# Turning a list schedule over, and squares' sums on VectorE alone, in a fused attention and GLU kernel

## The chip, the cores and the metric

The kernel runs on one core of one Trainium2 chip. The metric is device time in microseconds (us), the median over several executions. A core has a matrix engine (TensorE, PE), a vector engine (VectorE, DVE), an activation engine (ScalarE, ACT), GpSimd (POOL) and SyncE (SP), which here only issues transfers (DMAs). Each engine takes its instructions in the order in which the program lists them; they wait for one another through semaphores.

## The reference

The first part is attention over channels for 4 batches of 6080 tokens and 256 channels; the second a gated layer on its output with 2048 hidden channels.

```python
def _attn_ref(q, k, v, tau):
    qn = q / (np.linalg.norm(q, axis=1, keepdims=True) + 1e-06)
    kn = k / (np.linalg.norm(k, axis=1, keepdims=True) + 1e-06)
    s = kn.transpose(0, 2, 1) @ qn / tau
    s = s - s.max(-1, keepdims=True)
    a = np.exp(s)
    a /= a.sum(-1, keepdims=True) + 1e-09
    return (v @ a).astype(np.float32)

def _moe_ref(x, w_in, w_out):        # x: the rows of all batches
    h = x @ w_in
    g = h * (1.0 / (1.0 + np.exp(-1.702 * h)))
    return (g @ w_out).astype(np.float32)
```

`q`, `k`, `v` are float32, `w_in` and `w_out` arrive as 64-bit floats.

## The kernel before

The norms run over the tokens, so the scores of a batch need one pass over `q` and `k`, and the squares' sums of all columns come from the same pass. The softmax's 256x256 matrix is multiplied into `w_in`, so that each batch has its own weights (`weights`), and the long work is then one gated layer on `v`.

*The long work.* Tokens are cut into chunks of up to 1024, six for a batch. A chunk goes through 8 *pairs* of hidden blocks, so there are 4 x 6 x 8 = 192 pairs. A pair has a *front* (products of `w` and `v` into the PSUM banks X, Y, Z, copies of ACT that seed one bank from another, the gates) and a *back* (the gates' high and low parts `gi`, `gj`, `gr` times `wo`, `wb`, into the banks O2, O3, O4, O7 and K). Both use a scheme of seven products in the place of eight; every product is three matmuls, of high and low parts. The very first chunk has another division (`FIRST`) than the rest.

*Before it.* The 64-bit weights are converted on ACT and DVE (`win_convert`, `wout_convert`): the words of one piece are loaded into a buffer (the first ones into `ga0`, `ga1`, `gi0`, `gi1`, the 12 later ones all into `vr`, which `values` uses for `v` too), ACT copies, DVE puts the number together in several steps, and the result is stored to DRAM. Each buffer serves one user after another.

*Scores and squares.* `Attention.unit` handles 2 tiles of 128 tokens of `q` and `k`; a batch has 25 units. It loads them (`raw`), lets PE add to the scores, and lets ACT square them into a buffer `sq` (`gp` for batch 1), which is added into `acc`. Batches 0 and 1 are scored in float32 from `raw`; batches 2 and 3 load a second, rounded copy by POOL's queue (`hl`) and let DVE make the low part. In batch 0 the sum is split, half on DVE, half on POOL; in the other batches POOL issues a DMA that adds `sq` to `acc` (L498). Batch 0 is scored at the start and batch 1 beside the first chunk; batches 2 and 3 are spread over the pairs 19 to 60 and 74 to 118.

*The order.* Every step is a node with an engine, a cost, a *lag* after it (the time until a transfer has landed), what it depends on, the buffers that it uses, and a due time (`due`), worked out by hand from the pair's place. `Plan.order` places the nodes by their modelled times: on each engine, when it comes free, the ready node with the earliest due is next. A node of another engine is ready 60 ns after what it waits for, 165 ns more behind PE, and 350 ns more where PE itself waits. The nodes are then emitted by their start. A buffer's next user waits for all users of the one before. `load` costs 50 ns and 2.6 ns a KB on SP, with a lag of 3000 ns; `load_cast`, on POOL, 800 ns and the same lag.

Of the kernel before, what the change touches and what calls it, by code (L numbers as in the profile page):

```python
# [15 lines left out]
ALU = mybir.AluOpType  # L16
# [34 lines left out]
class Plan:  # L51

    DRAIN = {"PE": 165}
    MARGIN = {"PE": 350}
    HOP = 60

    def __init__(self):
        self.nodes = []  # L60
# [12 lines left out]
        self.nodes.append(n)  # L73
        return n

    def stuck(self):
        seen, path = set(), []
        n = next(n for n in self.nodes if n.start is None)
        while id(n) not in seen:
            seen.add(id(n))  # L80
            path.append((n.idx, n.eng, n.due, [getattr(b, "slot", "") for b in n.uses]))
            n = next(d for d in n.deps if (d.start is None if d.eng is not None else d.left))
        return path[-30:]

    def order(self):
        nodes = self.nodes
        free_of = {}
        extra = []
        for n in nodes:
            n.outs = []  # L90
        for n in nodes:
            deps = {id(d): d for d in n.deps}
            for b in n.uses:
                prev = b.prev
                while prev is not None and not prev.users:
                    prev = prev.prev
                if prev is not None:
                    r = free_of.get(id(prev))
                    if r is None:
                        r = Node(None, 0, None, prev.users, (), 0, 0, -1)  # L100
                        r.outs = []
                        free_of[id(prev)] = r
                        extra.append(r)
                    deps[id(r)] = r
            n.deps = list(deps.values())
        for n in nodes + extra:
            n.left, n.ready = len(n.deps), 0.0
            for d in n.deps:
                d.outs.append(n)
        engines = {n.eng for n in nodes}  # L110
        waiting = {e: [] for e in engines}
        avail = {e: [] for e in engines}
        free = {e: 0.0 for e in engines}
        events = []

        def arrive(n):
            heapq.heappush(waiting[n.eng], (n.ready, n.idx, n))
            heapq.heappush(events, (max(n.ready, free[n.eng]), n.eng))

        def done(n, end):  # L120
            for o in n.outs:
                if o.eng is None:
                    o.ready = max(o.ready, end)
                else:
                    t = end
                    if n.eng is not None and o.eng != n.eng:
                        t += self.DRAIN.get(n.eng, 0)
                    if n.eng != o.eng:
                        t += self.HOP + self.MARGIN.get(o.eng, 0)
                    o.ready = max(o.ready, t)  # L130
                o.left -= 1
                if o.left == 0:
                    if o.eng is None:
                        done(o, o.ready)
                    else:
                        arrive(o)

        for n in nodes:
            if n.left == 0:
                arrive(n)  # L140
        for r in extra:
            assert r.left
        placed = []
        while events:
            t, e = heapq.heappop(events)
            if free[e] > t:
                if waiting[e] or avail[e]:
                    heapq.heappush(events, (free[e], e))
                continue
            while waiting[e] and waiting[e][0][0] <= t:  # L150
                _, _, n = heapq.heappop(waiting[e])
                heapq.heappush(avail[e], (n.due, n.idx, n))
            if not avail[e]:
                continue
            _, _, n = heapq.heappop(avail[e])
            n.start = t
            placed.append(n)
            free[e] = t + n.cost
            done(n, t + n.cost + n.lag)
            if waiting[e] or avail[e]:  # L160
                heapq.heappush(events, (free[e], e))
        if len(placed) != len(nodes):
            raise AssertionError(self.stuck())
        return sorted(placed, key=lambda n: (n.start, n.idx))


def act(n, psum=False):
# [24 lines left out]
def channel_attention_then_glu(  # L192
# [10 lines left out]
    nc = tc.nc  # L203
# [18 lines left out]
    g = Plan()  # L222
# [34 lines left out]
    def plain(ap):  # L257
        return ap.bitcast(F32) if ap.dtype == F32R else ap

    def load(dst, src, kb, deps=(), uses=(), due=0.0):  # L260
        return g.add(
            "SP", 50 + kb * 2.6, lambda: nc.sync.dma_start(plain(dst()), plain(src())), deps, uses, due, lag=3000,
        )

    def load_cast(dst, src, kb, deps=(), uses=(), due=0.0):
        return g.add("POOL", 800, lambda: nc.gpsimd.dma_start(dst(), src()), deps, uses, due, lag=3000)

    def cast(dst, src, n, deps, uses, due, psum=False):
        return g.add("ACT", act(n, psum), lambda: nc.scalar.copy(dst(), src()), deps, uses, due)  # L269
# [4 lines left out]
    def tt(dst, a, b, op, n, deps, uses, due, eng="DVE"):  # L274
        if eng == "POOL":
            return g.add("POOL", pool(n), lambda: nc.gpsimd.tensor_tensor(dst(), a(), b(), op=op), deps, uses, due)
        return g.add("DVE", dve(n), lambda: nc.vector.tensor_tensor(dst(), a(), b(), op=op), deps, uses, due)  # L277
# [144 lines left out]
    class Attention:  # L422
# [39 lines left out]
        def unit(self, u, due, after=()):  # L462
            t0, nt, pp = self.units[u]
            if t0 not in self.raw:
                t = sbuf(f"ra{u % 2}", [P, 2, UT, C], F32, "raw")
                view = (lambda i: t()[:, i, :nt, :]) if pp == P else (lambda i: t()[:pp, i, 0, :])
                ns = [
                    load(
                        lambda i=i: view(i), lambda i=i: self.rows(i, t0, nt, pp), 128 * nt, after, [t], due - 8,
                    )  # L470
                    for i in range(2)
                ]
                for o in range(nt):
                    self.raw[t0 + o] = (t, o, ns)
            buf, o, _ = self.raw[t0]
            ready = [n for j in range(nt) for n in self.raw[t0 + j][2]]
            w = 2 * nt * C
            src = lambda: buf()[:pp, :, o : o + nt, :]
            acc = self.acc
            if u == 0:  # L480
                self.acc_n = [g.add(
                    "ACT", act(w), lambda: nc.scalar.activation(acc(), src(), AF.Square), ready, [buf, acc], due + 0.5,
                )]
            else:
                sq = sbuf("gp" if self.b == 1 else "sq", [P, 2, UT, C], F32, "sq")
                s = g.add(
                    "ACT", act(w),
                    lambda: nc.scalar.activation(sq()[:pp, :, :nt, :], src(), AF.Square), ready, [buf, sq], due + 1,  # L488
                )
                parts = [("DVE", slice(0, 1)), ("POOL", slice(1, 2))] if self.b == 0 else [("DMA", slice(0, 2))]  # L490
                new = []
                for e, (eng, sl) in enumerate(parts):
                    a = lambda sl=sl: acc()[:pp, sl, :nt, :]
                    more = lambda sl=sl: sq()[:pp, sl, :nt, :]
                    deps = [s, self.acc_n[min(e, len(self.acc_n) - 1)]]
                    if eng == "DMA":
                        new.append(g.add(
                            "POOL", 1200, lambda a=a, more=more: nc.gpsimd.dma_start(a(), more(), accum_op=ALU.add),  # L498
                            deps, [sq, acc], due + 1.5, lag=3500,
                        ))  # L500
                    else:
                        new.append(tt(a, a, more, ALU.add, w // len(parts), deps, [sq, acc], due + 1.5, eng))
                self.acc_n = new
            if self.direct:
                op, ok, uses = buf, ready, [buf]
            else:
                hl = sbuf("hl", [P, 2, UT, 2, C], F32R, "hl")
                hs = [
                    load_cast(
                        lambda i=i: hl()[:, i, :nt, 0, :] if pp == P else hl()[:pp, i, 0, 0, :],  # L510
                        lambda i=i: self.rows(i, t0, nt, pp), 128 * nt, after, [hl], due - 6,
                    )
                    for i in range(2)
                ]
                l = low(
                    lambda: hl()[:pp, :, :nt, 1, :], src, lambda: hl()[:pp, :, :nt, 0, :], w,
                    hs + ready, [buf, hl], due,
                )
                ok, uses = [l], [hl]
# [624 lines left out]
```

## Time and profile before

| | us |
|---|---|
| median of 3 runs | 2345.29 |
| lowest and highest | 2343.35, 2357.74 |
| the profiled execution | 2346.11 |
| its span, first to last instruction | 2344.4 |
| PE busy | 2184.9 (93%) |
| DVE busy | 1650.3 (70%) |
| ACT busy | 1583.5 (68%) |
| POOL busy | 179.3 (8%) |
| moved by DMA | 534.86 MB, mean 228 GB/s |

The page gives each engine's busy time and the chain of work that ended last; the table by stage gives the same busy times for stretches of the span, with the granted clock of PE as a share of 2.4 GHz. PE is the engine with most work, but not evenly: in the first 300 us its busy share is far below that of the end. Rows of the trace give the start of an instruction in us from the start of the span, its duration, and in brackets the idle time of its engine before it with what ended it.

### The profile page before, as it was taken

The numbers are of one execution on the slowest core, as the hardware profiler recorded it, in microseconds if no ns is written. First come the engines' busy times: TensorE is split into PE (matmuls) and PEld (weight loads), VectorE is DVE, ScalarE is ACT, GpSimd is POOL, SyncE is SP. The second block draws the span as 40 slices with busy tenths as digits, with TensorE's granted clock in tenths as the row PEclk, the third lists the DMA queues.
The fourth block names the chain that finished last, engine by engine and source line by source line (L and its number), as shares of the span: only waits on it lengthen the run. The fifth ranks groups of instructions, "written<-read, shape, count | busy, mean of one in ns | idle before, by whom it ended". The sixth has DMA issues, their size and how long they took to land.

```text
span 2344.4 us, 27182 instructions
## 1 busy us (share of the span) xinstructions
PE 2184.9 (93%) x9832; PEld 1789.5 (76%) x9832; DVE 1650.3 (70%) x2079; ACT 1583.5 (68%) x2309; POOL 179.3 (8%) x206
## 2 busy tenths in 40 slices
PE   8577699999999999999999999999999999999999
PEld 7455477778777777788787777778888878888887
DVE  6555477676766776877766777678777767767775
ACT  4454477667766676777666676677777777777775
POOL 4301100011111110001111111100000000000000
PEclk9798899999999999999999999999999999999999
DMA  8789867787878876678867878676766555645553
GB/s 287 220 255 270 266 221 250 243 267 235 267 225 255 254 202 207 243 257 266 262 207 245 250 227 257 204 228 215 265 225 215 172 189 193 215 158 203 199 178 127
DMA packets 205108, 534.86 MB, mean 228 GB/s; under 512 B 16688, under 2 KB 74672, under 8 KB 203952
## 3 DMA queue, kind: packets, MB, share of 16 engines
q1 hardware_dynamic: 168304, 472.44, 57.3%
q0 software_dynamic: 36672, 60.70, 12.7%
q8 instruction: 78, 1.28, 0.2%
q14 instruction: 54, 0.44, 0.1%
HBM read 430.44 MB, written 66.85 MB: 212 GB/s over the span
## 4 chain that ended last, share of the span: by engine, by line
PE 63%; DMA 20%; DVE 7%; ACT 6%; issue 2%; POOL 1%; SPq 1%; DVEq 0%; ACTq 0%
PE ps_o L767 21%; PE ps_X L767 12%; PE ps_k L767 9%; PE ps_Y L767 9%; PE ps_Z L767 8%; DMA acc<-sq 5%; DMA hl<-in_k 4%; DMA raw<-in_k 4%; PE ps_s L537 2%; DMA out_T<-oc 2%; ACT ga L793 2%; PE ps_w L684 2%; ACT sq L488 1%; DMA wi<-win_d 1%; DMA v_raw<-in_vT 1%
## 5 line engine op out<-in xcount | busy, mean ns | idle before, releaser
L767 PE MATMUL ps_X<-v,w 128*128 128x512 f32 (+1 forms) x1728 | 495.7, 395 | 14.4 <-ACT ps_Z L269 14.1
L767 PE MATMUL ps_o<-gi,wo 128*128 128x512 f32 (+1 forms) x1752 | 460.1, 389 | 1.7 <-DVE gi L292 1.7
L767 PEld LDWEIGHTS ps_X<-v,w 128*128 128x128 f32 x1728 | 322.7, 190 | 89.7 <-ACT ps_Z L269 29.2
L767 PEld LDWEIGHTS ps_o<-gi,wo 128*128 128x128 f32 x1752 | 328.4, 188 | 69.1 <-DVE gi L292 2.9
L767 PE MATMUL ps_Y<-v,w 128*128 128x512 f32 (+1 forms) x1152 | 331.9, 397 | 25.6 <-ACT ps_Y L269 22.5
L767 PE MATMUL ps_Z<-v,w 128*128 128x512 f32 (+1 forms) x1152 | 328.1, 392 | 22.8 <-ACT w L269 16.1
L793 ACT ACTIVATE ga<-ga 128x512 f32<-128x512 f32 (+1 forms) x384 | 232.9, 625 | 162.7 <-DVE ga L277 161.3
L767 PE MATMUL ps_o<-gj,wo 128*128 128x512 f32 (+1 forms) x1152 | 312.3, 396 | 14.4 <-DVE gj L283 5.4
L292 DVE TENSOR_TENSOR gi<-ga,gi 128x1536 fp32r<-128x1536 f32 (+2 forms) x192 | 280.6, 1462 | 49.3 <-ACT gi L269 48.4
L767 PEld LDWEIGHTS ps_Z<-v,w 128*128 128x128 f32 x1152 | 216.5, 189 | 75.3 <-ACT w L269 19.5
L767 PEld LDWEIGHTS ps_Y<-v,w 128*128 128x128 f32 x1152 | 216.9, 192 | 73.1 <-ACT ps_Y L269 26.8
L767 PEld LDWEIGHTS ps_o<-gj,wo 128*128 128x128 f32 x1152 | 216.6, 191 | 69.8 <-DVE gj L283 16.4
L277 DVE TENSOR_TENSOR ga<-ps_Y,m 128x512 f32<-128x512 f32 (+1 forms) x192 | 131.0, 682 | 183.6 <-PE ps_Y L767 149.1
L269 ACT CAST gi<-ga 128x1536 fp32r<-128x1536 f32 (+2 forms) x192 | 238.9, 1244 | 4.4
L488 ACT ACTIVATE sq<-raw 128x1024 f32<-128x1024 f32 (+1 forms) x96 | 98.2, 1023 | 181.7 <-DMA acc<-sq 73.5
L269 ACT COPY ps_Y<-ps_X 128x512 f32<-128x512 f32 (+1 forms) x192 | 109.3, 570 | 120.4 <-PE ps_X L767 119.2
L283 DVE SCALAR_TENSOR_TENSOR gj<-ga,gj 128x1024 fp32r<-128x1024 f32 (+1 forms) x100 | 121.2, 1212 | 76.4 <-ACT gj L852 76.0
L767 PE MATMUL ps_k<-gj,wo 128*128 128x512 f32 (+1 forms) x600 | 155.6, 390 | 2.6 <-DVE kc L277 1.8
L767 PE MATMUL ps_k<-gr,wb 128*128 128x512 f32 (+1 forms) x552 | 145.9, 388 | 0.0
L269 ACT COPY m<-ps_Z 128x512 f32<-128x512 f32 (+1 forms) x192 | 110.4, 575 | 39.1 <-PE ps_Z L767 39.0
L277 DVE TENSOR_TENSOR ga<-ps_X,m 128x512 f32<-128x512 f32 (+1 forms) x192 | 130.7, 681 | 5.6 <-PE ps_X L767 5.5
L793 ACT ACTIVATE ga<-ps_Y 128x512 f32<-128x512 f32 (+1 forms) x192 | 112.6, 587 | 30.3 <-PE ps_Y L767 29.4
(120 smaller groups left out, 2864.4 us busy)
## 6 DMA issues: line engine op xcount, KB each, us to landing
w<-w_d SPq DMA_DIRECT2D x184, 896.0 KB, 4.8
wo<-wout_d SPq DMA_DIRECT2D x92, 640.0 KB, 5.3
wo<-wout_d SPq DMA_DIRECT2D x100, 512.0 KB, 6.0
acc<-sq POOLq DMA_DIRECT2D x66, 512.0 KB, 5.9
wb<-wout_d SPq DMA_DIRECT2D x92, 256.0 KB, 4.1
w_d<-wst SPq DMA_DIRECT2D x24, 896.0 KB, 6.3
v_raw<-in_vT SPq DMA_DIRECT2D x20, 1024.0 KB, 8.7
out_T<-oc SPq DMA_DIRECT2D x80, 256.0 KB, 5.4
```

Of the source, the lines that this page charges most:

```text
L269: return g.add("ACT", act(n, psum), lambda: nc.scalar.copy(dst(), src()), deps, uses, due)
L277: return g.add("DVE", dve(n), lambda: nc.vector.tensor_tensor(dst(), a(), b(), op=op), deps, uses, due)
L283: lambda: nc.vector.scalar_tensor_tensor(dst(), in0=a(), scalar=-1.0, in1=b(), op0=ALU.mult, op1=ALU.subtract,),
L292: lambda: nc.vector.tensor_tensor(dst(), src(), hi().bitcast(F32), op=ALU.subtract),
L488: lambda: nc.scalar.activation(sq()[:pp, :, :nt, :], src(), AF.Square), ready, [buf, sq], due + 1,
L537: nc.tensor.matmul(out, lhsT=hl()[:pp, 1, j, l, ci], rhs=hl()[:pp, 0, j, r, :], start=begin and m == 0, stop=True, skip_group_check=True,)
L684: nc.tensor.matmul(pb()[:, i * 2 * P : (i + 1) * 2 * P], lhsT=at.aT()[:, l, j, ci], rhs=wi()[:, m, j, :], start=i == 0 and n == 0, stop=Tr ...
L767: nc.tensor.matmul(dst, lhsT=l(a), rhs=r(b), start=begin and n == 0, stop=True, skip_group_check=True,)
L793: lambda: nc.scalar.activation(dst(), src(), AF.Gelu_apprx_sigmoid, scale=sign), deps, uses, at,
```

## The change

Three things change, and the computation stays the same.

First, the order. `graph` now builds, once, the nodes with their incoming and outgoing arcs and the time of each arc (cost, lag, hops). `place` does the list placing for given arcs and a given key of priority. `order` places the nodes forwards with the dues as keys, as before, and then four times: backwards (arcs reversed, those that ended last first), and forwards again with the starts of the backward placing as keys. Of the five forward placings the one with the earliest end by the model is kept.

Second, the squares' sums: in all batches one add on VectorE over the whole unit, 1024 elements a partition, in the place of the halves on DVE and POOL (batch 0) and of the accumulating DMA (batches 1 to 3).

Third, the lags: 4000 ns for a load (5000 for the `raw` of a unit), 6000 for a `load_cast`; the dues of a unit's loads are 2 and 3 earlier.

```diff
+    TURNS = 4
...
+    def order(self):
+        nodes, ins, outs = self.graph()
+        cost = [n.cost for n in nodes]
+        back_ins = [[(b, w + cost[b] - cost[a]) for b, w in x] for a, x in enumerate(outs)]
+        back_outs = [[(a, w + cost[b] - cost[a]) for a, w in x] for b, x in enumerate(ins)]
+        start, end = self.place(nodes, ins, outs, [n.due for n in nodes])
+        best = (end, start)
+        for _ in range(self.TURNS):
+            back, end = self.place(nodes, back_ins, back_outs, [-t - c for t, c in zip(start, cost)])
+            start, end = self.place(nodes, ins, outs, [end - t - c for t, c in zip(back, cost)])
+            best = min(best, (end, start), key=lambda x: x[0])
+        for n, t in zip(nodes, best[1]):
+            n.start = t
+        return sorted(self.nodes, key=lambda n: (n.start, n.idx))
...
-    def load(dst, src, kb, deps=(), uses=(), due=0.0):
+    def load(dst, src, kb, deps=(), uses=(), due=0.0, lag=4000):
...
-        return g.add("POOL", 800, lambda: nc.gpsimd.dma_start(dst(), src()), deps, uses, due, lag=3000)
+        return g.add("POOL", 800, lambda: nc.gpsimd.dma_start(dst(), src()), deps, uses, due, lag=6000)
...
-                        lambda i=i: view(i), lambda i=i: self.rows(i, t0, nt, pp), 128 * nt, after, [t], due - 8,
+                        lambda i=i: view(i), lambda i=i: self.rows(i, t0, nt, pp), 128 * nt, after, [t], due - 10, 5000,
...
-                parts = [("DVE", slice(0, 1)), ("POOL", slice(1, 2))] if self.b == 0 else [("DMA", slice(0, 2))]
-                new = []
-                for e, (eng, sl) in enumerate(parts):
-                    a = lambda sl=sl: acc()[:pp, sl, :nt, :]
-                    more = lambda sl=sl: sq()[:pp, sl, :nt, :]
-                    deps = [s, self.acc_n[min(e, len(self.acc_n) - 1)]]
-                    if eng == "DMA":
-                        new.append(g.add(
-                            "POOL", 1200, lambda a=a, more=more: nc.gpsimd.dma_start(a(), more(), accum_op=ALU.add),
-                            deps, [sq, acc], due + 1.5, lag=3500,
-                        ))
-                    else:
-                        new.append(tt(a, a, more, ALU.add, w // len(parts), deps, [sq, acc], due + 1.5, eng))
-                self.acc_n = new
+                a = lambda: acc()[:pp, :, :nt, :]
+                self.acc_n = [tt(
+                    a, a, lambda: sq()[:pp, :, :nt, :], ALU.add, w, [s, *self.acc_n], [sq, acc], due + 1.5,
+                )]
...
-                        lambda i=i: self.rows(i, t0, nt, pp), 128 * nt, after, [hl], due - 6,
+                        lambda i=i: self.rows(i, t0, nt, pp), 128 * nt, after, [hl], due - 9,
```

## Rows read from the trace of the kernel before

**Rows 1.** The page: busy us (share) by engine; the last chain's shares.

```profile
PE 2184.9 (93%) x9832; PEld 1789.5 (76%) x9832; DVE 1650.3 (70%) x2079; ACT 1583.5 (68%) x2309; POOL 179.3 (8%) x206
...
PE 63%; DMA 20%; DVE 7%; ACT 6%; issue 2%; POOL 1%; SPq 1%; DVEq 0%; ACTq 0%
PE ps_o L767 21%; PE ps_X L767 12%; PE ps_k L767 9%; PE ps_Y L767 9%; PE ps_Z L767 8%; DMA acc<-sq 5%; DMA hl<-in_k 4%; DMA raw<-in_k 4%; PE ps_s L537 2%; DMA out_T<-oc 2%; ACT ga L793 2%; PE ps_w L684 2%; ACT sq L488 1%; DMA wi<-win_d 1%; DMA v_raw<-in_vT 1%
```

**Rows 2.** Table by stage: length, busy us (count) by engine, PE clock, DMA, GB/s.

```profile
80.00:300.00 220.00, 158.29 (x624) 121.30 (x625) 114.03 (x196) 102.17 (x147) 24.43 (x27) 0.86 0.87 257
...
440.00:900.00 460.00, 434.29 (x1986) 358.17 (x1987) 323.50 (x381) 312.10 (x451) 56.42 (x72) 0.98 0.78 238
...
1120.00:1560.00 440.00, 413.57 (x1891) 340.79 (x1890) 311.10 (x368) 297.25 (x433) 49.22 (x63) 0.98 0.77 238
1560.00:2344.40 784.40, 772.76 (x3456) 637.53 (x3455) 570.90 (x695) 569.78 (x848) 2.05 (x2) 1.00 0.56 196
```

**Rows 3.** Chain that ended last, 90 to 300 us: shares; start, us, what.

```profile
by line: DMA acc<-sq 59.3%; ACT sq L488 9.4%; issue 6.8%; DMA words<-in_w_in 6.6%; DMA wout_d<-cs 4.4%; DMA wo<-wout_d 2.4%; PE ps_o L767 2.0%; DMA words<-in_w_out 1.7%; PE ps_w L684 1.4%; PE ps_X L767 0.8%; PE ps_Y L767 0.6%; ACT L635 0.6%
...
170.15 4.55 DMA acc<-sq
...
271.86 11.07 DMA acc<-sq
```

**Rows 4.** Waits, 80 to 300 us (total, times, longest), and one PE row.

```profile
ACT sq L488 <- DMA acc<-sq: 73.5, 19, 7.6
...
187.47 1.65 PE L767 MATMUL ps_Y<-v,w 128*128 128x512 f32 x3 [5.36 <-ACT ps_Y L269]
```

**Rows 5.** SP's DMA issues, 80 to 300 us: first words, and the values.

```profile
86.66 0.43 SPq L262 DMA_DIRECT2D words<-in_w_in  x1
...
271.94 0.72 SPq L262 DMA_DIRECT2D v_raw<-in_vT  x1
```

**Rows 6.** The tile `words`: its DMAs, whole span.

```profile
DMA to landing us min/median/max: 2.9/7.2/10.0
```

**Rows 7.** A conversion: ACT's copies (80 to 300 us), DVE's first and last step.

```profile
L332 ACT ACTIVATE cv<-words 128x512 f32<-128x512 f32 x6 | 4.0, 666 | 2.7 <-DMA words<-in_w_in 2.7
...
242.02 0.43 DVE L337 TENSOR_SCALAR cv<-cv 128x512 f32<-128x512 f32 x1 [8.36 <-ACT cv L332]
...
244.13 0.69 DVE L363 SCALAR_TENSOR_TENSOR low<-words,low 128x512 f32<-128x512 uint32 x1
```

**Rows 8.** DVE, 80 to 300 us, two inputs of 1024: count, busy, mean ns.

```profile
L292 DVE TENSOR_TENSOR cs<-cf,cs 128x1024 fp32r<-128x1024 f32 x6 | 7.3, 1221 | 7.1 <-ACT cs L269 7.1
```

**Rows 9.** DMA, 80 to 300 us: POOL's queue; the sums to landing.

```profile
q0 software_dynamic: 3584, 11.93, 28.7%
...
acc<-sq POOLq DMA_DIRECT2D x22, 512.0 KB, 6.7
```

**Rows 10.** Squares' sums of batch 0 to 80 us; first and last `sq` of ACT.

```profile
L276 POOL TENSOR_TENSOR acc<-acc,sq 128x512 f32<-128x512 f32 x22 | 35.2, 1601 | 42.6 <-ACT sq L488 42.6
L277 DVE TENSOR_TENSOR acc<-acc,sq 128x512 f32<-128x512 f32 x22 | 23.6, 1073 | 12.3 <-ACT sq L488 12.3
...
8.59 1.06 ACT L488 ACTIVATE sq<-raw 128x1024 f32<-128x1024 f32 x1 [1.66 <-DMA raw<-in_k]
...
81.83 0.63 ACT L488 ACTIVATE sq<-raw 64x512 f32<-64x512 f32 x1 [0.90 <-DVE acc L277]
```

**Rows 11.** The tiles `hl` and `raw`: their DMAs, whole span.

```profile
DMA to landing us min/median/max: 3.1/6.5/10.8
DMA to landing us min/median/max: 2.1/5.2/11.1
```

**Rows 12.** Waits of PE and of ACT, 440 to 900 us.

```profile
PE ps_Y L767 <- ACT ps_Y L269: 6.7, 3, 3.7
PE ps_s L537 <- DMA hl<-in_k: 5.5, 2, 4.0
...
ACT sq L488 <- DMA raw<-in_k: 33.4, 16, 4.9
```

More of the change, by code (lines that the diff above doesn't have):

```diff
@@ L74, in add, with graph @@
         return n
[L76 to L86, printed above, removed]
+    def graph(self):
+        nodes = list(self.nodes)
         free_of = {}
[L88 to L91, printed above, removed]
+        for n in self.nodes:
             deps = {id(d): d for d in n.deps}
@@ L99, in order, with place @@
                     if r is None:
-                        r = Node(None, 0, None, prev.users, (), 0, 0, -1)
-                        r.outs = []
+                        r = Node(None, 0, None, prev.users, (), 0, 0, len(nodes))
                         free_of[id(prev)] = r
-                        extra.append(r)
+                        nodes.append(r)
                     deps[id(r)] = r
             n.deps = list(deps.values())
-        for n in nodes + extra:
-            n.left, n.ready = len(n.deps), 0.0
+        ins, outs = [[] for _ in nodes], [[] for _ in nodes]
+        for n in nodes:
             for d in n.deps:
-                d.outs.append(n)
-        engines = {n.eng for n in nodes}
+                w = d.cost + d.lag
+                if n.eng is not None and n.eng != d.eng:
+                    w += self.DRAIN.get(d.eng, 0) + self.HOP + self.MARGIN.get(n.eng, 0)
+                ins[n.idx].append((d.idx, w))
+                outs[d.idx].append((n.idx, w))
+        return nodes, ins, outs
+    @staticmethod
+    def place(nodes, ins, outs, key):
+        left = [len(x) for x in ins]
+        ready, start = [0.0] * len(nodes), [None] * len(nodes)
+        engines = {n.eng for n in nodes if n.eng is not None}
         waiting = {e: [] for e in engines}
@@ L114, in order, with done, arrive @@
         events = []
[L116 to L123, printed above, removed]
-                else:
[L125 to L143, printed above, removed]
+        def done(i, t):
+            start[i] = t
+            for o, w in outs[i]:
+                ready[o] = max(ready[o], t + w)
+                left[o] -= 1
+                if left[o] == 0:
+                    arrive(o)
+        def arrive(i):
+            e = nodes[i].eng
+            if e is None:
+                done(i, ready[i])
+                return
+            heapq.heappush(waiting[e], (ready[i], i))
+            heapq.heappush(events, (max(ready[i], free[e]), e))
+        for i, x in enumerate(ins):
+            if not x:
+                arrive(i)
         while events:
@@ L150, in order @@
             while waiting[e] and waiting[e][0][0] <= t:
-                _, _, n = heapq.heappop(waiting[e])
-                heapq.heappush(avail[e], (n.due, n.idx, n))
+                i = heapq.heappop(waiting[e])[1]
+                heapq.heappush(avail[e], (key[i], i))
             if not avail[e]:
                 continue
[L155 to L159, printed above, removed]
+            i = heapq.heappop(avail[e])[1]
+            free[e] = t + nodes[i].cost
+            done(i, t)
             if waiting[e] or avail[e]:
                 heapq.heappush(events, (free[e], e))
-        if len(placed) != len(nodes):
-            raise AssertionError(self.stuck())
-        return sorted(placed, key=lambda n: (n.start, n.idx))
+        assert None not in start
+        return start, max(t + n.cost for t, n in zip(start, nodes))
+    def order(self):
[12 more added lines that the diff above has]
+        return sorted(self.nodes, key=lambda n: (n.start, n.idx))
 def act(n, psum=False):
@@ L258, in plain @@
         return ap.bitcast(F32) if ap.dtype == F32R else ap
-    def load(dst, src, kb, deps=(), uses=(), due=0.0):
+    def load(dst, src, kb, deps=(), uses=(), due=0.0, lag=4000):
         return g.add(
-            "SP", 50 + kb * 2.6, lambda: nc.sync.dma_start(plain(dst()), plain(src())), deps, uses, due, lag=3000,
+            "SP", 50 + kb * 2.6, lambda: nc.sync.dma_start(plain(dst()), plain(src())), deps, uses, due, lag=lag,
         )
     def load_cast(dst, src, kb, deps=(), uses=(), due=0.0):
-        return g.add("POOL", 800, lambda: nc.gpsimd.dma_start(dst(), src()), deps, uses, due, lag=3000)
+        return g.add("POOL", 800, lambda: nc.gpsimd.dma_start(dst(), src()), deps, uses, due, lag=6000)
     def cast(dst, src, n, deps, uses, due, psum=False):
@@ L489, in unit @@
                 )
-                parts = [("DVE", slice(0, 1)), ("POOL", slice(1, 2))] if self.b == 0 else [("DMA", slice(0, 2))]
-                new = []
-                for e, (eng, sl) in enumerate(parts):
-                    a = lambda sl=sl: acc()[:pp, sl, :nt, :]
-                    more = lambda sl=sl: sq()[:pp, sl, :nt, :]
-                    deps = [s, self.acc_n[min(e, len(self.acc_n) - 1)]]
-                    if eng == "DMA":
-                        new.append(g.add(
-                            "POOL", 1200, lambda a=a, more=more: nc.gpsimd.dma_start(a(), more(), accum_op=ALU.add),
-                            deps, [sq, acc], due + 1.5, lag=3500,
-                        ))
-                    else:
-                        new.append(tt(a, a, more, ALU.add, w // len(parts), deps, [sq, acc], due + 1.5, eng))
-                self.acc_n = new
+                a = lambda: acc()[:pp, :, :nt, :]
+                self.acc_n = [tt(
+                    a, a, lambda: sq()[:pp, :, :nt, :], ALU.add, w, [s, *self.acc_n], [sq, acc], due + 1.5,
+                )]
             if self.direct:
```

## The prediction

> **What bounds the kernel now.** I read the page first. TensorE (PE) is busy 2184.9 of 2344.4 us, but the chain that ended last gives DMA 20% and one transfer, `acc<-sq`, 5% [rows 1]. So there are stages that PE does not set. The table by stage shows which [rows 2]. From 1560 us on PE is idle 11.6 of 784.4 us, the tail included, and does a matmul every 227 ns: nothing is to be had there but a loss. From 80 to 300 us it is idle 61.7 of 220 us, at a mean granted clock of 0.86 (of 2.4 GHz), and its matmuls take 254 ns each, though many are narrow ones. The two stretches in which the scores of batches 2 and 3 are made (440 to 900, 1120 to 1560) lose 25.7 and 26.4 us. So nearly all that can be won lies before 300 us and in these stretches.
>
> The chain from 90 to 300 us says why [rows 3]. It repeats: ACT squares a unit (1.06 us), POOL issues a DMA that adds the square to `acc`, the DMA lands 5 to 11 us later, and only then may ACT write the one `sq` buffer of this batch again. These transfers are 59.3% of that 210 us, 124.5 us. ACT takes its instructions in order, so behind a square that waits stand casts and gate functions that other work needs. The waits name it: 73.5 us of ACT behind `acc<-sq` in 19 places. One of them shows on PE: the copy `ps_Y<-ps_X` stands behind a square of ACT, and PE, idle for 5.36 us, starts at 187.47 [rows 4].
>
> What ends this stage is the chain of weight conversions through one buffer, `vr`: twelve `words` (6 of `w_in`, 6 of `w_out`), and behind them the values of the second chunk. The first is issued at 86.66 and the values at 271.94 [rows 5]: 185.3 / 12 = 15.4 us a conversion. From the trace a conversion needs its load (median 7.2 us to landing, fastest 2.9 [rows 6]), the ACT copy (0.67) and five VectorE (DVE) steps from 242.02 to 244.82, 2.8 us [rows 7]; with 0.9 for issue and handovers 4.4 us beside the load. At the median that is 11.6 us; the other 3.8 us of each are ACT behind squares.
>
> **The change, part by part.**
>
> *Sums of batches 1 to 3.* 72 accumulating DMAs and their POOL issues go; 72 adds on DVE come. The trace has no such add of 1024 elements; the nearest rows are `cs<-cf,cs` of the same width, 1.221 us [rows 8], so 24 x 1.22 = 29 us more DVE a batch. The chain's step falls from about 8 us (1.06, 0.3 to issue, 6.7 to land [rows 9]) to 1.06 + 1.22 and handovers, some 2.5 us, and no longer sets anything. The DMA engines lose a load as well: POOL's queue takes 28.7% of 16 engines' time from 80 to 300 us, all of it these sums, 63 us [rows 9].
>
> What is late next? With the ACT waits gone a conversion costs 4.4 us and its load. I keep the load at 7.2, since the same loads are pressed into less time, and add 0.6 us because DVE is fuller: 12.2 us, 146 for twelve, 39 less than now. Bounds: at the fastest landing of 2.9 it would be 7.3 us, 88 for twelve. But DVE has 114.0 us of work in the stage [rows 2] and gets 29 more; at 95% busy that needs 150 us, so no more than 70 of the 220 can go. At the other end the longest landing, 10.0 us, gives 15.0 us, 5 less in all. PE is not in the way: 158.3 us busy at a clock of 0.86 is about 136 at the full one, so the stage could be 40 to 60 us shorter for PE. I take -42, a little over the sum, since the other chains of the stage (weights, casts, gates) stood behind the same ACT waits.
>
> The Trainium skill, "DMA: Bandwidth & Descriptors", section on the anatomy of one DMA, fits a DMA of the GpSimd queue by 2.0 us plus its bytes at 436 GB/s, 3.2 us for 512 KB. The accumulating ones here took a median of 6.7 us to landing [rows 9], twice that, so the trace disagrees while the queues are full. If the `words` loads came down to that figure (an estimate, the fit being one for the other queue) twelve conversions would be 12 x 7.6 = 91 us and DVE's bound would decide, as at the fastest landing.
>
> *Sums of batch 0.* They lie between the loads and the first softmax. Squares start at 8.59 and the 24th at 81.83: 3.18 us each, where POOL's half takes up to 1.77 us (mean 1.60) and DVE's half 1.07 [rows 10]. Afterwards one DVE add of 1024. By the half's own mean it would take 2.15, the step 1.06 + 2.15 + 0.15 = 3.36 and the stage 4 us longer; by `cs` it takes 1.22 and the step is 2.43, 17 us shorter. I lean to `cs`, as DVE's half takes between 0.69 and 1.79 us and the long ones lie beside a POOL add, and POOL has none any more. Conversions on DVE lie between the adds, so I take 2.7: 23 x 0.48 = 11 us earlier, and the softmax and `vr` with it.
>
> The Trainium skill, "SBUF — State Buffer", section "Who interferes with whom", states that a DVE instruction with two SBUF inputs and a GpSimd instruction that reads SBUF hold each other up completely. That is what the long halves look like; by it the whole add takes 1.22 and the term is -11 to -17, without it +4.
>
> *Lags and dues.* The planner took 3.0 us for every load's landing. The raw loads show a median of 5.2 and the cast loads (`hl`) 6.5 [rows 11]; now it takes 5 and 6 (and 4 elsewhere), and asks for them 2 or 3 us sooner. In the score stretches ACT waits 33.4 us for `raw` in 16 squares, and PE's waits there are `ps_Y` behind ACT 6.7 us and `ps_s` behind `hl` 5.5, the two largest [rows 12]; the next stretch looks alike. If squares and scores are put later than their loads, much of the 52 us goes. Bounds: nothing, and -52. The accumulating DMAs do not show in these waits, so their removal gives little here; the adds bring DVE from 323.5 to 353 of 460 us [rows 2], 77%, still under PE. I take a third, -18.
>
> *The order.* Four times the planner places everything from the end backwards, takes those starts as the new priorities, places it forwards again, and keeps the order with the earliest end by its own costs. No instruction is added; what moves are all of them, SP's and POOL's issues too. In the steady stage it can gain at most 11.6 us less the tail. Before, the dues of back products stood 12 us later than the rest of their pair's; now an operand is wanted when the backward pass says, so leads can shrink. I cost it at nothing, hidden by ACT and DVE being busy 73% each there [rows 2]: they can run ahead as far as buffers allow. If that cover fails, PE waits once or twice a pair.
>
> **Sum.** The profiled execution took 2346.1 us (span 2344.4 and 1.7 around it), 0.8 above the median of the runs, 2345.3. 2346 - 11 - 42 - 18 = 2275; against the median about 2274.
>
> **Rivals.**
>
> *The turned order starves PE (the other side).* Place: the 184 pairs from the second chunk on, where `ps_X` and `ps_Y` wait for ACT's seeds and `ps_o` for DVE's lows. Price: 71 us of gain are used up at 0.39 us a pair, one late seed; at 0.6 us it costs 110 us and the time is 2385. For it: seeds are already the largest PE wait in the score stretches [rows 12]. Against: ACT and DVE durations are steady, and PE now idles under 0.2 us a pair from 1560 us.
>
> *The gain of the first 300 us goes to the next wait.* DMA from 80 to 300 us is 87% busy [rows 2]; if what is left lands no sooner and loads queue at 10 us, conversions stay at 15.0 us (-5). With -11 and another -5 to -15 from the rest the time is 2315 to 2325. For it: HBM traffic is unchanged. Against: 63 us of engine time leaves.
>
> *Loads land fast.* -70 by the DVE bound, -17 in batch 0, -35 in the score stretches: 2224.
>
> *The turning does nothing*: the first order stays the best by the planner's costs. Then sums and lags alone act, 2346 - 11 - 42 - 5 = 2288.
>
> **How the numbers follow.** My forecast 0.62 (its own range 2245 to 2305), the next wait 0.15, fast loads 0.10, the turning without effect 0.05, PE starved 0.08. A measurement of this kernel tells about 1% from no change, 23 us, so faster means under 2322. Faster: 0.62 + 0.10 + 0.05 and half of the next wait, 0.84; same 0.08, the other half; slower 0.08. The range from 2235 to 2325 leaves out the starved PE, half of the fast loads, and a part of the next wait's upper end, under 0.2.
>
> **What would show it.** Right: no `acc<-sq` DMA, no POOL add; ACT's waits for squares gone between 80 and 300 us, the granted clock there nearer 1, the values of the second chunk issued near 220 us instead of 272; the last square of batch 0 at 68 to 75 us; PE's share in the score stretches above 95.5%; PE still above 98% from then on. Wrong: conversions still at 14 us or more, DVE adds that wait long for squares with gate adds behind them, or PE idle in every pair of the steady stage.

## The result: 7.8% faster, more than twice what was forecast

The changed kernel takes 2167.7 us (median), the one before 2349.9 beside it; the ratio is 0.922 with an interval from 0.919 to 0.926. The forecast was 2274 with a range down to 2235. The profiled execution took 2164.1 us, its span 2162.3.

The page of the changed kernel: busy time by engine, then the last chain's shares.

```profile
PE 2120.8 (98%) x9832; PEld 1773.9 (82%) x9832; DVE 1723.5 (80%) x2151; ACT 1574.2 (73%) x2309; POOL 76.3 (4%) x110
...
PE 89%; DVE 4%; DMA 4%; ACT 2%; issue 1%; SPq 0%; POOL 0%; DVEq 0%; ACTq 0%
```

DMA fell from 20% of the chain to 4% and PE rose from 63% to 89% [rows 1]. The table by stage of the changed kernel, with the columns of [rows 2]:

```profile
80.00:300.00 220.00, 211.52 (x1008) 174.78 (x1007) 197.32 (x304) 167.98 (x246) 1.39 (x1) 1.00 0.83 294
...
440.00:900.00 460.00, 455.61 (x2153) 381.06 (x2152) 373.91 (x456) 338.68 (x500) 26.48 (x37) 1.00 0.69 232
...
1120.00:1560.00 440.00, 438.21 (x2064) 367.00 (x2063) 358.81 (x445) 327.30 (x484) 20.73 (x29) 1.00 0.69 234
1560.00:2162.30 602.30, 598.65 (x2670) 500.45 (x2668) 437.54 (x510) 438.09 (x655) 0.00 (x0) 1.00 0.55 189
```

Between 80 and 300 us PE does 1008 matmuls in the place of 624, at a granted clock of 1.00 (2.4 GHz) in the place of a mean of 0.86, and DVE does 197 us of work in the place of 114. But the two score stretches moved as well: 2153 for 1986 matmuls and 2064 for 1891 [rows 2]. Over the whole span the same 9832 matmuls keep PE busy for 2120.8 us in the place of 2184.9 [rows 1], and PE is idle for 41.5 us in the place of 159.5: a third of the gain, 64 us, lies inside PE's busy time. How far the kernel has come is best read from the loads of the chunks' values. SP's issues in the changed kernel, for the second, sixth, 13th and 19th chunk:

```profile
198.58 0.38 SPq L264 DMA_DIRECT2D v_raw<-in_vT  x1
...
501.10 0.40 SPq L264 DMA_DIRECT2D v_raw<-in_vT  x1
...
1114.39 0.39 SPq L264 DMA_DIRECT2D v_raw<-in_vT  x1
...
1624.90 0.55 SPq L264 DMA_DIRECT2D v_raw<-in_vT  x1
```

In the kernel before they were issued at 271.94 [rows 5], 613.04, 1258.71 and 1796.89. So it is 73 us ahead at the second chunk, 112 at the sixth, 144 at the 13th, 172 at the 19th, and 182 at the end. Up to the sixth chunk 39 us were won on top of the first 73, up to the 19th 60 more, in a stretch that holds most of the scores of batches 2 and 3, and 10 behind it.

### The profile page after: what moved, and what is told of

Its sections match the earlier page's. It is cut to its first block, busy times and chain, and to the rows that moved or that the text cites. A ratio compares the mean times of both kernels' runs of the same rounds, so it can differ in the third digit from the quotient of the medians.

```text
span 2162.3 us, 27041 instructions
## 1 busy us (share of the span) xinstructions
PE 2120.8 (98%) x9832; PEld 1773.9 (82%) x9832; DVE 1723.5 (80%) x2151; ACT 1574.2 (73%) x2309; POOL 76.3 (4%) x110
## 4 chain that ended last, share of the span: by engine, by line
PE 89%; DVE 4%; DMA 4%; ACT 2%; issue 1%; SPq 0%; POOL 0%; DVEq 0%; ACTq 0%
PE ps_o L759 29%; PE ps_X L759 17%; PE ps_k L759 14%; PE ps_Y L759 12%; PE ps_Z L759 11%; PE ps_s L529 3%; PE ps_w L676 2%; DMA w<-w_d 1%; DVE acc L279 1%; PE ps_s L523 1%; DMA hl<-in_k 1%; DMA words<-in_w_in 1%; ACT sq L490 0%; DVE gi L294 0%; DMA tau_sb<-in_tau 0%
## 5 line engine op out<-in xcount | busy, mean ns | idle before, releaser
L759 PE MATMUL ps_X<-v,w 128*128 128x512 f32 (+1 forms) x1728 | 486.3, 390 | 5.8 <-ACT ps_Z L271 3.5
L759 PE MATMUL ps_o<-gi,wo 128*128 128x512 f32 (+1 forms) x1752 | 465.8, 388 | 1.3 <-DVE gi L294 1.3
L759 PE MATMUL ps_Y<-v,w 128*128 128x512 f32 (+1 forms) x1152 | 324.5, 390 | 1.4 <-ACT ps_Y L271 1.4
L759 PE MATMUL ps_o<-gj,wo 128*128 128x512 f32 (+1 forms) x1152 | 305.2, 388 | 0.1
L279 DVE TENSOR_TENSOR gp<-ga 128x1024 f32<-128x1024 f32 (+1 forms) x92 | 111.4, 1211 | 37.2 <-ACT ga L785 35.3
```

What stands on the lines that cost most here:

```text
L759: nc.tensor.matmul(dst, lhsT=l(a), rhs=r(b), start=begin and n == 0, stop=True, skip_group_check=True,)
```

## The experiments

Each runs beside the kernel before; times are medians, and a ratio with its interval stands where it matters.

### The three parts, alone and together

Orders without turning have `TURNS = 0`; sums and lags are put back as in the diff.

```diff
-    TURNS = 4
+    TURNS = 0
```

> The kernel before with one part of the change: all squares' sums on VectorE; priorities by the hand-written dues, no turning, lags and dues as before. Theory A (ACT held up by the accumulating DMAs made most of the loss before 300 us, and the sums alone give it back): 2255 to 2280, with the values of the second chunk issued near 220 us, and the score stretches after 440 us as before. Theory B (the turned order is what gives the time): 2320 to 2345, the stage before 300 us hardly shorter.

> The kernel before with only the order turned over four times; squares' sums still split (batch 0) and by accumulating DMA (batches 1 to 3), old lags and dues. Theory A: the chain of 24 accumulating DMAs still stands, no less than about 8 us each, so before 300 us at most 20 to 40 us are won and the time is 2290 to 2320. Theory B: 2200 to 2240, since the order gives the time in all stages.

> The kernel before with only the new lags (4, 5 and 6 us) and the dues of a unit's loads 2 to 3 earlier; sums and order as before. If the lags empty the waits of the score stretches: 2300 to 2325, with ACT's waits for raw in 440 to 900 us falling from 33 us to under 10. If lags without a new order change little: 2335 to 2350.

> The changed kernel with the old lags and dues: order turned, sums on VectorE. Theory A: sums and order together give all before 300 us, the lags the score stretches, so 2190 to 2215. Theory B: 2165 to 2185, lags worth under 20 us.

> The changed kernel with no turning: sums on VectorE and new lags, order by the hand-written dues. Sums alone took 2256, lags alone cost 17 us, and lags on top of sums and order won 28. If longer lags hurt the order by dues whatever the sums: 2260 to 2280. If they hurt only while the accumulating DMAs stand: 2225 to 2250.

> The changed kernel with the sums as before (halves in batch 0, accumulating DMAs in batches 1 to 3): order turned and new lags. Order alone took 2302. If the lags help every turned order: 2270 to 2285. If with the chain of accumulating DMAs, whose lag stays at 3.5 us, longer lags of the rest do not help: 2295 to 2310.

| sums | order | lags | us | ratio to before |
|---|---|---|---|---|
| | | new | 2364.8 | 1.008 (1.006 to 1.011) |
| | turned | | 2302.0 | 0.981 (0.979 to 0.983) |
| | turned | new | 2292.1 | 0.977 (0.973 to 0.981) |
| VectorE | | | 2255.9 | 0.961 (0.959 to 0.964) |
| VectorE | | new | 2249.7 | 0.958 (0.954 to 0.962) |
| VectorE | turned | | 2195.1 | 0.935 (0.933 to 0.937) |
| VectorE | turned | new | 2167.7 | 0.922 (0.919 to 0.926) |

Of the two theories of the expectations, A's ranges came true in the three runs that they were given for (2255.9, 2302.0 and 2195.1) and B's in none; but A's "score stretches as before" does not hold, since the sums of batches 2 and 3 have a price of their own (below). The sums are the largest part, 92 us alone; the order gives 46 alone and 61 on top of the sums. The lags cost 17 us alone, which neither expectation had, give 6 (within the spread of the runs) beside the sums and 10 beside the order, between the two ranges there, and 27 beside both. They did what was expected of them at the place looked at: with the lags alone ACT's waits for `raw` in 440 to 1560 us fall from 57 to 13 us. But ACT then waits 26 us behind `acc<-sq`, where it had no such wait before, and PE's waits there rise from 57 to 65 us in all: those for `hl` from 10.0 to 14.3 us and for the seed in `ps_Z` from 7.1 to 12.1, while those for the seed in `ps_Y` fall from 14.3 to 6.8. A wait on ACT was no measure of what its end is worth. Beside both other parts PE waits 0.9 us for the landing of `hl` from 300 to 1600 us. The 26 us behind `acc<-sq` point at the accumulating DMAs; why the lags need both other parts was not settled.

### The sums, batch by batch

In the changed kernel the old form of the sum is put back for some batches only.

```diff
-                self.acc_n = [tt(
...
+                parts = [("DVE", slice(0, 2))] if self.b != 1 else [("DMA", slice(0, 2))]
...
```

So it stands for batch 1 (b1dma); b23dma takes the DMA for batches 2 and 3, and b0split the halves on VectorE and POOL for batch 0.

> The changed kernel, with batch 0's sums split again between VectorE and POOL; batches 1 to 3 on VectorE. The prediction put this part at 11 us (bounds 17 less, 4 more): 2175 to 2185. If VectorE, now at 86% or more before 300 us, was better off with half the adds on POOL: 2160 or less.

> The changed kernel with the accumulating DMAs back in batch 1 alone. The prediction put this part at 42 us. If that was the size: 2205 to 2215. If the parts add up (12 for batch 0, 35 for batches 2 and 3, of 124 in all): 77 us, 2240 to 2250, all of it lost before 300 us.

> The changed kernel, with the accumulating DMAs back in batches 2 and 3 alone. The prediction said that their removal gives little in the score stretches: 2165 to 2175. If they were what made the loads of these stretches late (16% of the DMA engines' time there), as the fall of the loss after 300 us by sums alone suggests (from 136 to 111 us): 2185 to 2210, with hl and raw landing later and PE waiting at the scores.

Batch 0 split again: 2179.8, 12 us more. DMA in batch 1: 2242.0, 74 more. DMA in batches 2 and 3: 2202.8, 35 more. Together 121 us, and all of them at once cost 124 (2292.1). The parts add up. For batch 1 the waits of 80 to 300 us (total, times, longest) show the old picture [rows 4]:

```profile
ACT sq L490 <- DMA acc<-sq: 74.6, 21, 6.9
```

### Batch 1: the squares' place, or the chain

If ACT's squares were only listed too early, a planner that knows how long the accumulating DMA takes would list them later and free ACT.

```diff
-                            deps, [sq, acc], due + 1.5, lag=3500,
+                            deps, [sq, acc], due + 1.5, lag=7500,
```

> Order turned, new lags, sums as before, and the accumulating DMA's lag in the planner 7.5 us in the place of 3.5, near what it takes. With the false lag it took 2292. If the harm was that ACT's squares were listed too early and stood in front of other work: 2220 to 2260. If the serial chain of 24 such DMAs, about 8 us each, itself ends the stage (batch 1 must be done before the second chunk's buffers are free): 2280 to 2295.

> The kernel before with only that lag changed, 3.5 to 7.5 us; order by the dues. Squares listed too early: 2290 to 2320. The chain itself: 2335 to 2355.

2300.8 with the turned order (2292.1 with the false lag) and 2361.0 with the order by dues: no gain, both even a little above the ranges for the chain. Yet ACT was freed in part. In the turned one its waits behind `acc<-sq` from 80 to 300 us fell from 86.0 to 44.1 us, and the values of the second chunk were issued at 219 us, 53 earlier than in the kernel before. What stayed is the chain itself. The chain that ended last in that kernel, 230 to 340 us (start, us, what):

```profile
279.57 1.06 ACT sq L490
280.64 0.28 issue
280.92 4.56 DMA acc<-sq
285.57 1.07 ACT sq L490
286.92 7.43 DMA acc<-sq
...
317.94 3.27 DMA acc<-sq
```

and its table by stage:

```profile
80.00:200.00 120.00, 97.28 (x417) 79.21 (x418) 87.40 (x154) 69.98 (x103) 11.88 (x13) 0.87 0.90 288
200.00:260.00 60.00, 48.97 (x203) 38.84 (x202) 33.83 (x52) 31.45 (x44) 4.31 (x5) 0.89 0.88 274
260.00:350.00 90.00, 38.35 (x134) 28.22 (x132) 21.05 (x37) 27.65 (x39) 9.26 (x10) 0.72 0.53 133
```

PE is well used to 260 us and then has little: it is busy 38 of 90 us while the last nine sums follow one another. The second chunk needs buffers that batch 1 holds (`gr0`, `gr1`, `gp`, `wb`), so its back cannot begin before the 24 sums, some 9.6 us each from 91 to 321 us, are through.

This run alone does not part the squares' place from the chain, for the chain grew with the lag: 22 us in all now pass between the landings and the squares behind them, 1 us with the false lag, and the last sum lands at 321 instead of 299 us. What ties the time to the chain is the first use of `gp` by the second chunk. In the seven kernels with accumulating DMAs in batch 1 it follows the landing of the last sum by 12 to 21 us, whether the values were issued at 219 or at 272 us. The first such row in the kernel before, in o_acclag, in b1dma and in the changed kernel:

```profile
313.97 1.23 DVE L277 TENSOR_TENSOR gp<-ga 128x1024 f32<-128x1024 f32 x1 [0.70 <-ACT ga L793]
336.01 1.23 DVE L279 TENSOR_TENSOR gp<-ga 128x1024 f32<-128x1024 f32 x1
302.66 1.23 DVE L279 TENSOR_TENSOR gp<-ga 128x1024 f32<-128x1024 f32 x1
228.75 1.22 DVE L279 TENSOR_TENSOR gp<-ga 128x1024 f32<-128x1024 f32 x1
```

The last sum lands at 295, 321 and 286 us in the first three. From b1dma to the changed kernel `gp` comes 74 us earlier, and 74 us is what batch 1's DMAs cost. So the serial chain set the time of this stage.

### Batches 2 and 3: DMA time, POOL's queue, or the chain

The sums stay on VectorE, and a transfer that nobody reads is added for each square: two plain stores to DRAM on SP's queue, or one accumulating DMA into a spare tile from POOL's.

```diff
+                if self.b >= 2:
+                    g.add(
+                        "POOL", 1200, lambda: nc.gpsimd.dma_start(
+                            spare()[:pp, :, :nt, :], sq()[:pp, :, :nt, :], accum_op=ALU.add,
+                        ),
+                        [s, spare_n], [sq], due + 1.5, lag=3500,
+                    )
```

> The changed kernel with all sums on VectorE, and for batches 2 and 3 two plain stores of each square to a spare DRAM tile on SP's queue, which nobody reads: about the DMA engines' time of the accumulating DMA (3 us of 16 engines a unit), without POOL's queue and without the chain. If that time makes the 35 us that accumulating DMAs cost in batches 2 and 3: 2190 to 2210. If POOL's queue or the squares' wait makes it: 2165 to 2180.

> The changed kernel with all sums on VectorE, and for batches 2 and 3 an accumulating DMA of each square into a spare SBUF tile, which nobody reads, from POOL's queue: the DMA time and POOL's queue behind the square, no wait of the sums. If POOL's queue counts beside the DMA time: 2190 to 2210, and more than with the plain stores. If only the wait of the sums for one another counts: 2165 to 2180.

2192.3 (25 us more than without) and 2208.6 (41 more); the true accumulating DMAs cost 35. So no wait of one sum for another is needed for the loss. The DMA views from 440 to 1500 us (share of 16 engines; then count, KB each, median us to landing), first with the plain stores, then with the spare accumulation:

```profile
q1 hardware_dynamic: 92887, 261.52, 70.1%
q0 software_dynamic: 22656, 21.76, 8.5%
...
hl<-in_k POOLq DMA_DIRECT2D x40, 256.0 KB, 8.1
```

```profile
q1 hardware_dynamic: 77753, 211.53, 57.4%
q0 software_dynamic: 29248, 43.52, 19.6%
...
hl<-in_k POOLq DMA_DIRECT2D x40, 256.0 KB, 6.6
```

The changed kernel has 59.9%, 8.5% and 5.9 us there, the one with the true sums (b23dma) 58.0%, 19.7% and 7.5 us. Both fillings take about as much of the engines, 10 and 11% more. With the stores `hl` lands later; with POOL's transfers it lands only a little later, yet the kernel loses more. There POOL stands 601 us behind squares before it may issue anything else, and its wait for PE's scores, which is what should free it, falls from 587 to 112 us: the next cast loads are behind the square in its queue. POOL's waits from 440 to 1500 us, in the changed kernel and then with the spare accumulation:

```profile
POOL hl L268 <- PE ps_s L529: 587.0, 34, 23.0
POOL spare_t L504 <- ACT sq L496: 601.0, 41, 26.2
POOL hl L270 <- PE ps_s L542: 112.4, 26, 18.9
```

With the true sums they are 570 and 110 us. So the traffic and the place in POOL's queue both count as far as these runs go. How much each makes of the 35 us is not shown: the plain stores bring waits of their own (SP stands 89 us behind squares before it may issue them, and ACT 18 us behind their landing before it may square again), and the two fillings are not quite alike.

### The order: whose, how many turns, and chance

A further forward placing with mixed keys, one set of engines by the hand-written dues:

```diff
+        key = [d if n.eng == "PE" else k for n, d, k in zip(nodes, due, best[2])]
+        start, end = self.place(nodes, ins, outs, key)
```

> The changed kernel, but with one more forward placing whose keys are mixed: TensorE's instructions by the hand-written dues again, all other engines by the turned keys. The turned order is worth 82 us (2250 to 2168). If it is what VectorE and ScalarE do first that counts, since PE waited for lows of VectorE under the dues: 2168 to 2195. If PE's own order counts: 2220 to 2250.

> The other half: VectorE and ScalarE by the hand-written dues, TensorE, POOL and SP by the turned keys. If the order of VectorE and ScalarE counts: 2220 to 2250, with PE waiting for gj, gi and ss again. If PE's order counts: 2168 to 2195.

2207.4 with PE by the dues (40 us lost of the 82 that turning is worth), 2223.9 with VectorE and ScalarE by the dues (56 lost). The first lies between its two ranges. Neither half of the keys keeps the worth, so it lies in lists that fit together; 17 us between two single orders do not show which half weighs more. PE's waits from 300 to 1600 us (total, times, longest), with no turning and then turned, sums and lags being the same:

```profile
PE ps_X L759 <- ACT ps_Z L271: 7.3, 11, 1.2
PE ps_Z L759 <- DVE ss L279: 6.9, 7, 1.3
PE ps_o L759 <- DVE gj L285: 5.9, 9, 0.9
PE ps_k L759 <- DVE gi L294: 5.7, 6, 1.1
PE ps_o L759 <- DVE gi L294: 3.7, 6, 0.8
```

```profile
PE ps_X L759 <- ACT ps_Z L271: 3.4, 3, 1.6
PE ps_s L529 <- DVE hl L294: 1.4, 2, 1.0
PE ps_o L759 <- DVE gi L294: 1.3, 2, 1.1
```

Under the dues PE stood 22 us behind four kinds of DVE work (`ss`, `gj`, and `gi` twice); in the turned order only 1.3 us of it is left among the longest. With VectorE and ScalarE put back to the dues, `ss` (6.2 us) and `gi` (4.7) are at the top again.

Any change of the planner's inputs gives another order of everything, so chance had to be sized.

```diff
-    MARGIN = {"PE": 350}
+    MARGIN = {"PE": 600}
```

> The changed kernel with the planner's margin in front of TensorE 600 ns in the place of 350: a slightly other order of everything. It shows how much of a difference between two turned orders is chance: within 8 us of 2168 if such orders are alike, more than 15 us off if a small change of the planner's inputs already moves the time by as much as single engines' keys did.

> The changed kernel with the planner's margin in front of TensorE 340 ns in the place of 350: too little to mean anything, yet another turned order. If a turned order is worth what it is by its rule: 2160 to 2180. If it is one draw among orders that a planner's end does not tell apart: more than 15 us off, as with 600 ns (2225).

> The changed kernel with one turn (backwards and forwards once) in the place of four. If one turn gives most and the others little: 2168 to 2185. If each turn adds: 2195 to 2225, between the order by dues (2250) and four turns (2168).

340 ns gives another order and 2166.2 us, 0.923 (0.921 to 0.924), the same as the changed kernel's within a measurement. That is one draw: it speaks against chance as the source of the 40 and 56 us, and does not size it. For 600 ns takes 2224.8, 57 more, as much as single engines' keys did. PE then waits for ACT's seed 17.7 us from 300 to 1600 us where it waited 3.4:

```profile
PE ps_X L759 <- ACT ps_Z L271: 17.7, 14, 2.3
```

That is 14 of the 57 us. Whether the margin's size makes the rest, or the order that came of it, is not shown. One turn in the place of four takes 2177.0: 73 of the 82 us come with the first. No kernel tried was measurably faster than the changed one.

## Why the prediction was wrong, point by point

**What ends the stage before 300 us.** The prediction named the conversions through `vr`, with ACT behind squares as what slows them. Both are in the trace, but this step failed: the second chunk waited for the end of batch 1's chain of sums, whose last one lands at 295 us, 23 us after the values were issued, and with the conversions freed (o_acclag) the chain alone held the time. The prediction priced this chain only by the waits of ACT and gave its end no price. The change removes both, so the direction was right.

**The size of that term, -42 (batch 1).** It measured 74, as much as `gp` came earlier. In the prediction's own sum the term that was mis-sized is the load: 7.2 us were kept because the same loads would be pressed into less time. They landed sooner. And 7.2 is a median over the whole span and two sizes: from 80 to 300 us the loads of `w_in` (512 KB) took 7.8 us and those of `w_out` (256 KB) 8.6, which leaves less than the 3.8 us of a conversion to ACT's squares. The tile `words` in the changed kernel, its DMAs over the whole span:

```profile
DMA to landing us min/median/max: 2.5/5.0/8.0
```

With 5.0 and the 4.4 and 0.6 us of the prediction a conversion takes 10.0; it took (198.58 - 73.16) / 12 = 10.5. The accumulating DMAs were themselves what made the loads late: with them back in batch 1 alone the median is 6.7 us. The bound of 70 us was drawn too tight too: DVE's work was summed to 300 us, while the next chunk's values were issued at 272. From 80 to 200 us DVE is busy 113 of 120 us in the changed kernel, so that it comes near its bound was right. By the fit of the Trainium skill ("DMA: Bandwidth & Descriptors", section on the anatomy of one DMA), which is one for GpSimd's queue, 512 KB would take 3.2 us. The loads on SP's queue do not show that: from 70 us on those of 512 KB take a median of 5.3 us in the changed kernel, and only those of 256 KB take 3.2.

**Batch 0, -11.** It measured 12; size and mechanism were right. Its squares now come every 2.35 us where nothing lies between, and the 24th starts at 68.42 where it started at 81.83. The add costs what `cs` did [rows 8], and not twice the half [rows 10]; all 88 adds of 1024 elements in the changed kernel (count, busy, mean ns, idle before):

```profile
L279 DVE TENSOR_TENSOR acc<-acc,sq 128x1024 f32<-128x1024 f32 x88 | 107.3, 1219 | 20.9 <-ACT sq L490 20.7
```

The Trainium skill ("SBUF — State Buffer", "Who interferes with whom") states that a DVE instruction with two SBUF inputs contends with a GpSimd instruction that reads SBUF. The trace agrees: without POOL's adds the whole add takes 1.219 us. In the kernel before, DVE's half took 0.69 us in 14 units, in which it started before POOL's half or found none running, and 1.67 to 1.79 us in the 8 in which POOL's half had started first, as in these two pairs:

```profile
12.73 0.69 DVE L277 TENSOR_TENSOR acc<-acc,sq 128x512 f32<-128x512 f32 x1 [1.18 <-ACT sq L488]
12.78 1.77 POOL L276 TENSOR_TENSOR acc<-acc,sq 128x512 f32<-128x512 f32 x1 [1.78 <-ACT sq L488]
...
21.59 1.43 POOL L276 TENSOR_TENSOR acc<-acc,sq 128x512 f32<-128x512 f32 x1 [1.17 <-ACT sq L488]
21.82 1.75 DVE L277 TENSOR_TENSOR acc<-acc,sq 128x512 f32<-128x512 f32 x1
```

**Batches 2 and 3, "their removal gives little here".** It gave 35 us. The step that failed is reading worth off the name of a wait: `acc<-sq` stands in none of PE's waits there, but its packets made `hl` and `raw` land later (from 440 to 1500 us the medians of the loads of `k` rise from 5.9 to 7.5 and from 5.4 to 6.3 us when the DMAs are put back in these two batches) and its instruction stood in front of the next cast load on POOL. The queue table had a sign of it all along: POOL's queue takes 25.1% of the engines' time from 440 to 900 us before and 8.2% after.

```profile
q0 software_dynamic: 15921, 23.79, 25.1%
...
q0 software_dynamic: 9152, 8.78, 8.2%
```

**The lags, -18.** 27 us in this company, but 17 lost alone. The argument, waits of ACT that longer lags would end, describes something that happened and, alone, paid nothing. That -18 lies near 27 is in part luck.

**The order, at nothing.** This is the largest error: 82 us beside the other two parts. The step that failed is the term of nothing: its reason, that ACT and DVE, busy 73% each, can run ahead, was read in the steady stage, and for the stages before 1560 us the prediction gave none. Against the kernel without turning (s_sums_lags) the worth is spread over the whole span: the values of the second, sixth, 13th and 19th chunk are issued 12, 31, 50 and 72 us earlier, and the end comes 84 us earlier. Of these 84 us 35 lie inside PE's busy time, at nearly the same granted clock (a mean of 0.993 and 0.995). The page of s_sums_lags, to be held against 2120.8 us in the changed kernel:

```profile
PE 2155.6 (96%) x9832; PEld 1766.9 (79%) x9832; DVE 1717.7 (76%) x2151; ACT 1582.3 (70%) x2309; POOL 76.9 (3%) x110
```

The prediction looked for gain only where PE was named idle, and in the steady stage, where its bound of 11.6 us held: from the 19th chunk on the changed kernel is 10 us faster than the one before. Its loss in the score stretches was read as idle time alone, 52 us. Now PE does 8.4% more matmuls in the first score stretch (2153 for 1986, with 316 narrow ones, of 256 columns or fewer, for 282) and 9.1% more in the second (280 narrow ones for 246), where its idle share was 5.6 and 6.0%. The counts would have told: at the prediction's own 227 ns for a wide matmul and 133 ns for a narrow one, an estimate from 24 of 256 columns that keep PE busy for 3.2 us between 1700 and 1900 us in the kernel before, the two stretches lose 36 and 34 us. What makes PE's busy time longer there is not shown. (The 227 ns include idle time and the 254 ns that the prediction puts beside them do not.)

**The rivals.** The starved PE did not come: from 1560 us PE is idle 3.7 us. The gain did not go to the next wait. The turning did something. Fast loads were nearest, 2224, and still 56 us too high. Nearly all signs that were named for a right forecast came true (a granted clock of 1.00 before 300 us, the values at 199, the last square of batch 0 at 68 us, PE's share at 99% or more in the score stretches), so they told the direction and not the size.

## What to carry to other kernels

The transfers that accumulate were paid for here in three ways: as a serial chain whose end held buffers, as traffic beside which other loads land later, and as an instruction in front of its queue; look for all three before costing such a removal by the wait that bears its name. Where engines run fixed lists, worth lies in how the lists fit together: a backward placing for priorities beat hand-written due times, and one turn gave most of it. Count matmuls in a stretch as well as its idle time: both the whole change and the order alone shortened PE's busy time too. The planner's constants matter: a margin of 600 ns in the place of 350 gave back two thirds of what turning had won, for reasons seen only in part, and longer lags lost time alone and won it beside the other two parts.

## What the runs showed of the hardware that was not expected

By an estimate from the queue tables, an accumulating DMA of 512 KB from SBUF to SBUF takes about twice the DMA engines' time of a plain store of the same size to DRAM. From 440 to 1500 us POOL's queue goes from 8.5 to 19.6% with some 40 of them: 0.111 x 1060 / 40 = 2.9 us of all 16 engines each. The plain stores raise SP's queue from 59.9 to 70.1% with some 80: 0.102 x 1060 / 80 = 1.4 us each. The 22 of batch 1 before 300 us, alone on POOL's queue but for two smaller ones, agree: 0.287 x 220 / 22 = 2.9 us [rows 9].
